# Folding the token mixing's gain and bias into the weights: one multiply from PSUM in place of a bias operation and a multiply

## The chip, the cores and the metric

The kernel runs on one core of a Trainium2 chip. The metric is the device time of one execution in microseconds (us). Most executions of one kernel agree within some tenths of a per cent, so medians of several runs are compared, and a run that is more than 1.5% above the fastest of its kernel counts as slow and is left out of the ratios.

The engines are called PE (matrix multiplies), PEld (PE's weight loads), DVE (vector), ACT (scalar), POOL (GpSimd) and SP (it issues most transfers). PE writes to PSUM; DVE and ACT read PSUM or SBUF; POOL works in SBUF here. The *granted clock* of PE is the share of its full clock that it was given, as the profile shows it.

## The reference

A retention layer (attention without softmax, with a decay per head) feeds a gated MLP whose gate mixes tokens. Shapes: batch 8, 8 heads, 576 tokens, head size 64, so the model size is 512 and the MLP's half width is 512.

```python
# retention: x[b, t, :] = sum_{s<=t} gamma_h^(t-s) (q_t . k_s)/sqrt(64) v_s, heads side by side
h = gelu_tanh(x @ w_in);  u, v = halves of h
v_n = (v - mean(v)) / sqrt(var(v) + 1e-6) * g_ln
v_s = einsum('ts,bsd->btd', w_sg, v_n) + b_sg[None, :, None]
out = x + (u * v_s) @ w_out                  # float32
```

What matters: `g_ln` scales a feature and `b_sg` is added to a token. With S = w_sg · normalised v, the gated value is u · (g_f S_tf + b_t).

## The kernel before

The 8 × 576 tokens are cut into 36 tiles of 128. Two batch items make nine tiles, so the fifth tile of each pair (`m == MID`) holds 64 tokens of either item. The mixing matrix is transposed once into `wT[e][j]`, with zero rows where the shared tile holds the other item's tokens. The retention of tile i+1, the projections of tile i and, from a work list, two pieces of "later" work run in each step: a piece is one token mixing (`mlp_W`, 32 pieces, four feature blocks for each item) or one output projection (`mlp_O`, 36 pieces).

```python
def prep(i):                                             # POOL: casts and decay-scaled values
    nc.gpsimd.tensor_copy(qkb[:], qk[:]...)              # f32 -> bf16, 128x1024
    for hh in range(2):
        nc.gpsimd.tensor_tensor(vp[...], vf[...], gv[...], op=Alu.mult)
    ...
def mlp_V(i):
    ...                                                  # hv on PE, vg = gelu on ACT, statistics on DVE and POOL
    vn = vnp.tile([128, F2], BF, name="vn")
    nc.scalar.activation(vn[:], vg[:], Act.Identity, scale=rs[:], bias=nm[:])
    vns[i] = vn
    ...
def mlp_W(b, c):
    ...
    ps = [psD.tile([128, HS], F32, name="wp", tag="d") for _ in range(2)]
    for j in range(SB):                                  # 5 token tiles
        for half in range(2):
            nc.tensor.matmul(ps[half][:], vns[t0 + j][:, 128 * c:128 * c + 128],
                             wT[e][j][:, half * HS:(half + 1) * HS],
                             start=(j == 0), stop=(j == SB - 1))
    for half in range(2):
        col = e * S + half * HS
        vs = work.tile([128, HS], BF, name="vs")
        nc.vector.scalar_tensor_tensor(vs[:], ps[half][:], g_col[:, c:c + 1],
                                       b_bc[:, half * HS:(half + 1) * HS],
                                       op0=Alu.mult, op1=Alu.add)
        nc.vector.tensor_tensor(gTs[p][:, c, col:col + HS], vs[:], uTs[p][:, c, col:col + HS], op=Alu.mult)
    ...
def mlp_O(i):
    ...                                                  # op = gT @ w_out + x, on PE
    nc.scalar.activation(ob[:], op[:], Act.Copy)         # ACT empties PSUM
    nc.scalar.dma_start(outf[128 * i:128 * i + 128, :], ob[:])
```

The three PSUM buffers of `psD` are shared by hv, hu, wp and op. In names: sc holds the scores of a tile and ret their masked form; vpad holds v with its decay; zp and zbd are the state that goes from one tile to the next; xT is the retention's result, transposed. hu and hv are the halves of x @ w_in before gelu, uT and vg after it; nm, rs and vn belong to the normalisation; wp is a mixing, op an output projection.

Of the kernel before, what the change touches and what calls it, by code (L numbers as in the profile page):

```python
# [11 lines left out]
F32 = mybir.dt.float32  # L12
BF = mybir.dt.bfloat16
I32 = mybir.dt.int32
Act = mybir.ActivationFunctionType
Alu = mybir.AluOpType
# [3 lines left out]
def kernel(  # L20
# [12 lines left out]
    nc = tc.nc  # L33
    B, H, S, D = q.shape
    DM = H * D
    F2 = moe_w_in.shape[1] // 2
    KK = H // 2
    NT = 2 * S // 128
    NP = B // 2
    MID = NT // 2  # L40
    HS = S // 2
    SB = (S + 127) // 128
# [4 lines left out]
    consts = ctx.enter_context(tc.tile_pool(name="consts", bufs=1))  # L47
    ld = ctx.enter_context(tc.tile_pool(name="ld", bufs=5))
    work = ctx.enter_context(tc.tile_pool(name="work", bufs=4))
    pairp = ctx.enter_context(tc.tile_pool(name="pairp", bufs=2))  # L50
    vnp = ctx.enter_context(tc.tile_pool(name="vnp", bufs=14))
    psA = ctx.enter_context(tc.tile_pool(name="psA", bufs=1, space=bass.MemoryType.PSUM))
    psS = ctx.enter_context(tc.tile_pool(name="psS", bufs=2, space=bass.MemoryType.PSUM))
    psD = ctx.enter_context(tc.tile_pool(name="psD", bufs=3, space=bass.MemoryType.PSUM))
# [12 lines left out]
    def load(i):  # L67
        p, m = divmod(i, NT)
        qk = ld.tile([128, 2, H, D], F32, name="qk", tag="qk")
        vf = ld.tile([128, H, D], F32, name="vf")  # L70
        for (p0, b, r0, n) in segs(m):
            bb = 2 * p + b
            nc.sync.dma_start(qk[p0:p0 + n, 0, :, :], q[bb, :, r0:r0 + n, :].transpose([1, 0, 2]))
            nc.sync.dma_start(qk[p0:p0 + n, 1, :, :], k[bb, :, r0:r0 + n, :].transpose([1, 0, 2]))
            nc.sync.dma_start(vf[p0:p0 + n, :, :], v[bb, :, r0:r0 + n, :].transpose([1, 0, 2]))
        loaded[i] = (qk, vf)
# [4 lines left out]
    w_in = consts.tile([128, KK, 2 * F2], BF, name="w_in")  # L81
    w_out = consts.tile([128, KK, DM], BF, name="w_out")
    wnat = consts.tile([128, SB, S + 128], BF, name="wnat")
    b_bc = consts.tile([128, S], F32, name="b_bc")
    g_col = consts.tile([128, KK], F32, name="g_col")
    w_stage = []
    for half in (1, 0):
        for c in (0, 2):
            wst = ld.tile([128, 2, F2], F32, name="wst", tag="qk")
            nc.sync.dma_start(wst[:], moe_w_in.rearrange("(c p) f -> p c f", p=128)[:, c:c + 2, half * F2:(half + 1) * F2])  # L90
            w_stage.append((half, c, wst))
        load(1 if half else 2)
    nc.sync.dma_start(b_bc[:], moe_b_sg.partition_broadcast(128))
    nc.sync.dma_start(g_col[:], moe_g_ln.rearrange("(c p) -> p c", p=128))


    ident = consts.tile([128, 128], BF, name="ident")
# [6 lines left out]
    NB0 = S - 128 * MID  # L104
# [36 lines left out]
    kbds = [consts.tile([128, KK, 2, 128], BF, name=f"kbd{i}") for i in range(NK)]  # L141
    zbds = [consts.tile([128, KK, 128], BF, name=f"zbd{i}") for i in range(NZ)]
    kmid = consts.tile([128, H * D], BF, name="kmid")
    for t in vpads[:1] + kbds[:1] + vpads[1:] + kbds[1:] + zbds:
        nc.vector.memset(t[:], 0.0)
    nc.vector.memset(kmid[:NB0, :], 0.0)

    def load_w():
        nc.gpsimd.memset(wnat[:, :, 0:64], 0.0)
        nc.gpsimd.memset(wnat[:, :, 64 + S:], 0.0)  # L150
        for j in range(SB):
            n = min(128, S - 128 * j)
            nc.gpsimd.dma_start(wnat[:n, j, 64:64 + S], moe_w_sg[128 * j:128 * j + n, :])
        nc.gpsimd.dma_start(w_out[:], moe_w_out.rearrange("(c p) f -> p c f", p=128))


    wT = [[consts.tile([128, S], BF, name=f"wT{e}_{j}") for j in range(SB)] for e in range(2)]
# [11 lines left out]
    xTs, uTs, gTs = {}, {}, {}  # L169
    zp = {}  # L170

    def prep(i):
        p, m = divmod(i, NT)
        qk, vf = loaded.pop(i)
        qkb = work.tile([128, 2, H * D], BF, name="qkb")
        nc.gpsimd.tensor_copy(qkb[:], qk[:].rearrange("p a h d -> p a (h d)"))  # L176
        vp = vpads[i % NV]
        for hh in range(2):
            nc.gpsimd.tensor_tensor(
                vp[:].rearrange("p (k g) c -> p k g c", g=2)[:, :, hh, hh * 64:hh * 64 + 64],  # L180
                vf[:].rearrange("p (k g) d -> p k g d", g=2)[:, :, hh, :],
                gv[:, m, :].rearrange("p (k g) -> p k g", g=2)[:, :, hh].unsqueeze(2).to_broadcast([128, KK, 64]),
                op=Alu.mult)
        if m == MID:
            nc.gpsimd.tensor_copy(kmid[NB0:, :], qk[NB0:, 1, :, :].rearrange("p h d -> p (h d)"))
        st[i] = dict(qkb=qkb, vp=vp)
# [73 lines left out]
    vns = {}  # L260

    def mlp_V(i):
        p, m = divmod(i, NT)
        hv = psD.tile([128, F2], F32, name="hv", tag="d")
        for kk in range(KK):
            nc.tensor.matmul(hv[:], xTs[p][:, kk, 128 * m:128 * m + 128], w_in[:, kk, F2:],  # L266
                             start=(kk == 0), stop=(kk == KK - 1))
        vg = work.tile([128, F2], F32, name="vg")
        nc.scalar.activation(vg[:], hv[:], Act.Gelu_apprx_tanh)  # L269
        bst = work.tile([128, 6], F32, name="bst")  # L270
        nc.vector.bn_stats(bst[:], vg[:])  # L271
        mv = work.tile([128, 2], F32, name="mv")
        nc.vector.bn_aggr(mv[:], bst[:])  # L273
        rs = work.tile([128, 1], F32, name="rs")
        nc.gpsimd.tensor_scalar(rs[:], mv[:, 1:2], 1e-6, None, op0=Alu.add)  # L275
        nc.gpsimd.tensor_tensor(rs[:], rs[:], mhalf[:], op=Alu.pow)  # L276
        nm = work.tile([128, 1], F32, name="nm")
        nc.gpsimd.tensor_scalar(nm[:], mv[:, 0:1], rs[:], -1.0, op0=Alu.mult, op1=Alu.mult)  # L278
        vn = vnp.tile([128, F2], BF, name="vn")
        nc.scalar.activation(vn[:], vg[:], Act.Identity, scale=rs[:], bias=nm[:])  # L280
        vns[i] = vn

    def mlp_U(i):
        p, m = divmod(i, NT)
# [10 lines left out]
    def mlp_W(b, c):  # L295
        p, e = divmod(b, 2)
        if e == 0 and c == 0:
            gTs[p] = pairp.tile([128, KK, NT * 128], BF, name="gT")
        t0 = NT * p + (MID if e else 0)
        ps = [psD.tile([128, HS], F32, name="wp", tag="d") for _ in range(2)]  # L300
        for j in range(SB):
            for half in range(2):
                nc.tensor.matmul(ps[half][:], vns[t0 + j][:, 128 * c:128 * c + 128],  # L303
                                 wT[e][j][:, half * HS:(half + 1) * HS],
                                 start=(j == 0), stop=(j == SB - 1))
        for half in range(2):
            col = e * S + half * HS
            vs = work.tile([128, HS], BF, name="vs")
            nc.vector.scalar_tensor_tensor(vs[:], ps[half][:], g_col[:, c:c + 1],  # L309
                                           b_bc[:, half * HS:(half + 1) * HS],  # L310
                                           op0=Alu.mult, op1=Alu.add)
            nc.vector.tensor_tensor(gTs[p][:, c, col:col + HS], vs[:], uTs[p][:, c, col:col + HS], op=Alu.mult)  # L312

    def mlp_O(i):
        p, m = divmod(i, NT)
        op = psD.tile([128, DM], F32, name="op", tag="d")
        r = slice(128 * m, 128 * m + 128)
        for c in range(KK):
            nc.tensor.matmul(op[:], gTs[p][:, c, r], w_out[:, c, :], start=(c == 0), stop=False,  # L319
                             skip_group_check=True)  # L320
        for kk in range(KK):
            nc.tensor.matmul(op[:, 128 * kk:128 * kk + 128], xTs[p][:, kk, r], ident[:],  # L322
                             start=False, stop=True, skip_group_check=True)
        ob = work.tile([128, DM], F32, name="ob")
        nc.scalar.activation(ob[:], op[:], Act.Copy)  # L325
        nc.scalar.dma_start(outf[128 * i:128 * i + 128, :], ob[:])  # L326
# [5 lines left out]
    def run(n):  # L332
        for _ in range(n):
            if wo:
                wo.pop(0)()
# [7 lines left out]
    def flush(i):  # L343
        while waiting and waiting[0][0] <= i:
            b = waiting.pop(0)[1]
            p, e = divmod(b, 2)
            lo = NT * p + (MID if e else 0)
            for c in range(KK):
                wo.append(lambda b=b, c=c: mlp_W(b, c))
            for m in range(MID + e):  # L350
                wo.append(lambda i=lo + m: mlp_O(i))
# [9 lines left out]
    wbuild = [(e, j) for e in range(2) for j in range(SB)]  # L361
    for i in range(N + 3):
        flush(i)
        if i + 4 < N:
            load(i + 4)
        if i + 2 < N:
            prep(i + 2)
        if i < N:
            attn_S(i)
        if 1 <= i <= N:  # L370
            mlp_V(i - 1)
            release(i - 1)
        if i >= 2 and wbuild:
            build_wT(*wbuild.pop(0))
            build_wT(*wbuild.pop(0))
        if i + 1 < N:
            attn_T(i + 1)
        if 1 <= i <= N:
            mlp_U(i - 1)
        if i < N:  # L380
            attn_O(i)
            attn_Z(i)
        run(2)
# [31 lines left out]
```

## Time and profile before

| Before | |
|---|---|
| time, median of the first 3 runs | 283.47 us (282.51 to 283.56) |
| profiled span | 280.1 us, mean granted PE clock 0.982 |
| busy | PE 225.7, DVE 204.5, ACT 127.5, POOL 126.2 us |
| 12 steps with two mixings, while input work goes on ("W steps") | 84.27 us, 7.02 each |
| 12 steps with two projections | 78.46 us, 6.54 each |
| 3 steps with one projection | 17.05 us |
| seventh xT write, where the first mixings come in | at 66.50 us |
| last xT write, then the drain | at 257.85 us, 22.2 us |

A *step* is the time from one xT write on DVE to the next, read off the timeline; its kind is given by the gT writes in it. Steps let one cut the span where different things limit it.

Busy times by engine (first part of the page of the kernel before; us, share of the span, instructions):

```profile
PE 225.7 (81%) x2462; PEld 171.4 (61%) x2498; DVE 204.5 (73%) x451; ACT 127.5 (46%) x226; POOL 126.2 (45%) x240
```

No engine is busy for the whole span, so the total alone does not name a limit. A window of two W steps does. The columns are busy time with the number of records for each engine, then the granted PE clock, the transfers' share and their rate (windows of the kernel before; the first line heads the columns):

```profile
core 0: us, PE busy (x) PEld busy (x) DVE busy (x) ACT busy (x) POOL busy (x), PEclk, DMA share, GB/s
125.98:140.82 14.84, 11.72 (x131) 9.07 (x131) 14.78 (x32) 5.36 (x9) 8.81 (x15) 1.00 1.13 196
```

DVE is busy 14.78 of 14.84 us: these steps are DVE's. This pair is heavier than the mean of 7.02 us a step; over all twelve W steps DVE is busy 83.8 of 84.27 us. (PE's 131 records are fewer than the 144 matmuls that two such steps issue: the weight loads, of which none is missing, number 131 too, so PE had run ahead of xT and did most of the others before the window. Of hv's eight matmuls the trace has six.)

The costliest groups on DVE (page of the kernel before; line, engine, operation, tiles and shapes, count, then busy us and mean ns, then idle time just before them and what ended it):

```profile
L212 DVE TENSOR_TENSOR ret<-sc,tri 128x512 bf16<-128x512 f32 x64 | 40.9, 678 | 6.5 <-PE sc L210 6.5
...
L309 DVE SCALAR_TENSOR_TENSOR vs<-wp,g_col,b_bc 128x288 bf16<-128x288 f32 x64 | 29.8, 503 | 2.8 <-PE wp L303 2.6
...
L312 DVE TENSOR_TENSOR gT<-vs,uT 128x288 bf16<-128x288 bf16 x64 | 28.1, 477 | 0.0
```

The gate's multiply, gT, has a mean of 477 ns, but the mean hides two populations. The view of the tile gT gives minimum, median and maximum:

```profile
L312 DVE TENSOR_TENSOR gT<-vs,uT x64: 289/301/1144, 67.5 to 271.7; 128x288 bf16<-128x288 bf16 x64
```

The slow ones are found where POOL reads SBUF. First DVE's timeline, then POOL's, for the same stretch (start us, duration us, engine, line, operation; x2 is two instructions drawn as one):

```profile
187.26 0.92 DVE L309 SCALAR_TENSOR_TENSOR vs<-wp,g_col,b_bc 128x288 bf16<-128x288 f32 x2
188.12 1.36 DVE L312 TENSOR_TENSOR gT<-vs,uT 128x288 bf16<-128x288 bf16 x2
```

```profile
187.64 1.03 POOL L176 CAST qkb<-qk 128x1024 bf16<-128x1024 f32 x1
188.65 1.30 POOL L179 TENSOR_TENSOR vpad_157<-vf,gv 128x256 bf16<-128x256 f32 x2
```

Two multiplies that take 0.51 us elsewhere (at 163.46 us in the same trace; their records overlap a little) take 1.36 us beside POOL's cast and multiplies; vs, whose second tensor is in SBUF but whose first is in PSUM, keeps its 0.92 us for two. The Trainium skill, "SBUF — State Buffer", section "Who interferes with whom", says that a DVE instruction with two SBUF inputs contends with a GpSimd instruction that reads SBUF, and that one with at most one SBUF input (outside the two-port modes) does not. The trace agrees.

How DVE's load reaches PE is in the waits (kernel before; who waited for whom, us in total, times, longest):

```profile
PE wp L303 <- DVE vs L309: 7.7, 11, 1.0
```

### The profile page before, as it was taken

To read this page: it belongs to the slowest core of one execution; us is meant where nothing else is said; L and a number is where in the kernel's file an instruction comes from. 1 tells how busy PE (TensorE), PEld (TensorE's weight loads), DVE (VectorE), ACT (ScalarE), POOL (GpSimd) and SP (SyncE) were. 2 spreads that over 40 slices of the span, in tenths; PEclk is the share of its full clock that TensorE was granted. 3 is DMA by queue.
4 is the path that set the end of the run, shared out by engine and by line. 5 is a ranking of instruction groups with operands and counts; after the bars stand their busy time and mean duration, and the time that the engine had idled before them with its cause. 6 is when DMAs were issued, how large, how long until landed. Compare 5 with 4: busy or idle time off the path is not lost.

```text
span 280.1 us, 6362 instructions
## 1 busy us (share of the span) xinstructions
PE 225.7 (81%) x2462; PEld 171.4 (61%) x2498; DVE 204.5 (73%) x451; ACT 127.5 (46%) x226; POOL 126.2 (45%) x240
## 2 busy tenths in 40 slices
PE   0428773879889889986898799887997999889894
PEld 0216553657667667765676577666766777667562
DVE  7826672749996797579965997679876986599170
ACT  1632443223346536553455345563356455644613
POOL 5923518057455545646615665365634561111200
PEclk9999996879999999999999999999999999999999
DMA  8999999993005896699939897799945002200304
GB/s 183 256 282 196 169 201 205 224 208 77 21 0 148 205 211 155 152 257 211 186 97 220 159 202 189 195 172 170 205 130 136 0 2 80 90 23 1 116 37 187
DMA packets 120670, 41.74 MB, mean 149 GB/s; under 512 B 113792, under 2 KB 114880, under 8 KB 120640
## 3 DMA queue, kind: packets, MB, share of 16 engines
q1 hardware_dynamic: 114272, 30.71, 57.0%
q10 hardware_dynamic: 5184, 9.44, 9.1%
q0 software_dynamic: 1184, 1.19, 2.5%
q8 instruction: 19, 0.31, 0.5%
q14 instruction: 11, 0.09, 0.1%
HBM read 33.08 MB, written 9.44 MB: 152 GB/s over the span
## 4 chain that ended last, share of the span: by engine, by line
DVE 39%; PE 24%; ACT 10%; DMA 7%; POOL 7%; issue 6%; SPq 3%; ACTq 2%; POOLq 0%; DVEq 0%
DVE gT L312 7%; DVE ret L212 7%; DVE vs L309 7%; PE op L319 7%; DVE bst L271 5%; ACT ob L325 5%; DMA vf<-in_v_dram 5%; DVE xT L234 4%; ACT vg L269 3%; PE hv L266 3%; PE hu L290 2%; ACTq L326 2%; PE ot L230 2%; PE sc L210 2%; PE wp L303 2%
## 5 line engine op out<-in xcount | busy, mean ns | idle before, releaser
L275 POOL TENSOR_SCALAR rs<-mv 128x1 f32<-128x1 f32 x36 | 8.0, 221 | 114.7 <-DVE mv L273 114.6
L280 ACT ACTIVATE vn<-vg,nm,rs 128x512 bf16<-128x512 f32 x36 | 29.3, 814 | 55.1 <-POOL nm L278 55.1
L271 DVE BATCH_NORM_STATS2 bst<-vg 128x6 f32<-128x512 f32 x36 | 24.7, 687 | 30.7 <-ACT vg L269 30.7
L212 DVE TENSOR_TENSOR ret<-sc,tri 128x512 bf16<-128x512 f32 x64 | 40.9, 678 | 6.5 <-PE sc L210 6.5
L290 PE MATMUL hu<-xT,w_in 128*128 128x128 bf16 x576 | 38.7, 220 | 4.5 <-ACT ob L325 3.8
L303 PEld LDWEIGHTS <-vn 128*128 128x128 bf16 x320 | 30.2, 97 | 19.3 <-issue 11.7
L176 POOL CAST qkb<-qk 128x1024 bf16<-128x1024 f32 x36 | 37.3, 1035 | 9.2 <-DMA qk<-in_k_dram 6.4
L266 PE MATMUL hv<-w_in,xT 128*128 128x512 bf16 x123 | 36.8, 390 | 4.8 <-DVE xT L234 2.7
L290 PEld LDWEIGHTS <-w_in 128*128 128x128 bf16 x576 | 34.7, 98 | 7.4 <-issue 5.8
L269 ACT ACTIVATE vg<-hv 128x512 f32<-128x512 f32 x36 | 21.5, 596 | 37.4 <-PE hv L266 30.5
L319 PE MATMUL op<-w_out,gT 128*128 128x512 bf16 x129 | 35.9, 379 | 0.6
L309 DVE SCALAR_TENSOR_TENSOR vs<-wp,g_col,b_bc 128x288 bf16<-128x288 f32 x64 | 29.8, 503 | 2.8 <-PE wp L303 2.6
L193 PE MATMUL tp<-ident,qkb 128*128 128x128 bf16 x288 | 23.9, 230 | 9.3 <-POOL qkb L176 9.3
L193 PEld LDWEIGHTS <-qkb 128*128 128x128 bf16 x288 | 20.2, 103 | 17.3 <-POOL qkb L176 9.7
L312 DVE TENSOR_TENSOR gT<-vs,uT 128x288 bf16<-128x288 bf16 x64 | 28.1, 477 | 0.0
L293 ACT ACTIVATE uT<-hu 128x512 bf16<-128x512 f32 x36 | 21.3, 590 | 11.3 <-PE hu L290 11.3
L325 ACT ACTIVATE ob<-op 128x512 f32<-128x512 f32 x36 | 20.9, 591 | 11.2 <-PE op L322 7.5
L234 DVE TENSOR_TENSOR xT<-ot,ttab 128x512 bf16<-128x512 f32 x36 | 24.4, 677 | 1.6 <-PE ot L230 1.0
L195 DVE COPY qT<-tp 128x512 bf16<-128x512 bf16 x36 | 14.8, 412 | 11.3 <-PE tp L193 11.1
L276 POOL TENSOR_TENSOR rs<-rs,mhalf 128x1 f32<-128x1 f32 x36 | 20.4, 566 | 2.8
L266 PEld LDWEIGHTS <-xT 128*128 128x128 bf16 x144 | 12.6, 101 | 12.1 <-DVE xT L234 3.9
L319 PEld LDWEIGHTS <-gT 128*128 128x128 bf16 x144 | 12.6, 98 | 8.6
(109 smaller groups left out, 432.8 us busy)
## 6 DMA issues: line engine op xcount, KB each, us to landing
out_dram<-ob ACTq DMA_DIRECT2D x36, 256.0 KB, 2.4
qk<-in_q_dram SPq DMA_DIRECT2D x32, 256.0 KB, 5.1
qk<-in_k_dram SPq DMA_DIRECT2D x32, 256.0 KB, 5.0
vf<-in_v_dram SPq DMA_DIRECT2D x32, 256.0 KB, 5.0
wst<-in_moe_w_in_dram SPq DMA_DIRECT2D x4, 512.0 KB, 8.5
qk<-in_q_dram SPq DMA_DIRECT2D x8, 128.0 KB, 4.8
qk<-in_k_dram SPq DMA_DIRECT2D x8, 128.0 KB, 4.6
vf<-in_v_dram SPq DMA_DIRECT2D x8, 128.0 KB, 4.4
```

What stands on the lines that cost most here:

```text
L176: nc.gpsimd.tensor_copy(qkb[:], qk[:].rearrange("p a h d -> p a (h d)"))
L193: nc.tensor.transpose(tp[:, a, kk, :], s["qkb"][:, a, kk * 128:(kk + 1) * 128], ident[:])
L212: nc.vector.tensor_tensor(ret[:, 4 * j:4 * j + 4, :], sc[:], msk[:].unsqueeze(1).to_broadcast([128, 4, 128]), op=Alu.mult)
L234: nc.vector.tensor_tensor(xTs[p][:, :, 128 * m:128 * m + 128], ot[:], ttab[:, :, t0:t0 + 128], op=Alu.mult)
L266: nc.tensor.matmul(hv[:], xTs[p][:, kk, 128 * m:128 * m + 128], w_in[:, kk, F2:], start=(kk == 0), stop=(kk == KK - 1))
L271: nc.vector.bn_stats(bst[:], vg[:])
L290: nc.tensor.matmul(hu[:, c, :], w_in[:, kk, 128 * c:128 * c + 128], xTs[p][:, kk, 128 * m:128 * m + 128], start=(kk == 0), stop=(kk == KK ...
L303: nc.tensor.matmul(ps[half][:], vns[t0 + j][:, 128 * c:128 * c + 128], wT[e][j][:, half * HS:(half + 1) * HS], start=(j == 0), stop=(j == ...
L309: nc.vector.scalar_tensor_tensor(vs[:], ps[half][:], g_col[:, c:c + 1], b_bc[:, half * HS:(half + 1) * HS], op0=Alu.mult, op1=Alu.add)
L312: nc.vector.tensor_tensor(gTs[p][:, c, col:col + HS], vs[:], uTs[p][:, c, col:col + HS], op=Alu.mult)
L319: nc.tensor.matmul(op[:], gTs[p][:, c, r], w_out[:, c, :], start=(c == 0), stop=False, skip_group_check=True)
L325: nc.scalar.activation(ob[:], op[:], Act.Copy)
```

## The change

Intent: u·(g S + b) = g·u·(S + b/g). The factor g goes into the rows of `w_out`, once, at the start. The term b_t/g_f is a product of a column of 1/g and a row of b, so PE can add it as part of the mixing: the shared tile has zero rows in its contraction, and four of them are filled with b on the side of `wT` and 1/g on the side of `vn`. Four, because both numbers are split into a bf16 part and the bf16 rest, and all four products are summed. The shared tile therefore needs a normalised copy for each of the two items (`vmid`), each with its own four rows. What is left of the gating on DVE is one multiply that reads the mixing straight from PSUM.

```diff
-    vnp = ctx.enter_context(tc.tile_pool(name="vnp", bufs=14))
+    vnp = ctx.enter_context(tc.tile_pool(name="vnp", bufs=10))
 ...
-    nc.sync.dma_start(b_bc[:], moe_b_sg.partition_broadcast(128))
+    nonzero(g_col[:], g_tmp[:])                      # 3 DVE ops: |g| < 1e-20 becomes 3e-20
 ...
+    def build_rows():                                # called at step i == SB
+        nonzero(row4[:, 0, :F2], row_t[:, :F2])
+        nc.vector.reciprocal(row4[:, 0, :F2], row4[:, 0, :F2])
 ...                                                  # bf16 part or rest, by row, into row4b
+        for t in vmid:
+            nc.sync.dma_start(t[0][NB0:NB0 + 4, :], row4b[:, 0, :F2])
+            nc.sync.dma_start(t[1][0:4, :], row4b[:, 0, :F2])
+        nc.sync.dma_start(wT[0][SB - 1][NB0:NB0 + 4, :], row4b[:, 1, :])
+        nc.sync.dma_start(wT[1][0][0:4, :], row4b[:, 1, :])
 ...
-        nc.gpsimd.dma_start(w_out[:], moe_w_out.rearrange("(c p) f -> p c f", p=128))
+        for c in (0, 2):
+            wst = ld.tile([128, 2, F2], F32, name="wst", tag="qk")
+            nc.sync.dma_start(wst[:], moe_w_out.rearrange("(c p) f -> p c f", p=128)[:, c:c + 2, :])
+            for r in range(2):
+                nc.vector.tensor_scalar(w_out[:, c + r, :], wst[:, r, :], g_col[:, c + r:c + r + 1], None, op0=Alu.mult)
 ...
-        vn = vnp.tile([128, F2], BF, name="vn")
-        nc.scalar.activation(vn[:], vg[:], Act.Identity, scale=rs[:], bias=nm[:])
-        vns[i] = vn
+        if m == MID:
+            vns[i] = vmid[p % 2]
+            for e, sl in ((0, slice(0, NB0)), (1, slice(NB0, 128))):
+                nc.scalar.activation(vns[i][e][sl, :], vg[sl, :], Act.Identity, scale=rs[sl, :], bias=nm[sl, :])
+        else:
+            vn = vnp.tile([128, F2], BF, name="vn")
+            nc.scalar.activation(vn[:], vg[:], Act.Identity, scale=rs[:], bias=nm[:])
+            vns[i] = [vn, vn]
 ...
-            vs = work.tile([128, HS], BF, name="vs")
-            nc.vector.scalar_tensor_tensor(vs[:], ps[half][:], g_col[:, c:c + 1],
-                                           b_bc[:, half * HS:(half + 1) * HS],
-                                           op0=Alu.mult, op1=Alu.add)
-            nc.vector.tensor_tensor(gTs[p][:, c, col:col + HS], vs[:], uTs[p][:, c, col:col + HS], op=Alu.mult)
+            nc.vector.tensor_tensor(gTs[p][:, c, col:col + HS], ps[half][:], uTs[p][:, c, col:col + HS], op=Alu.mult)
```

## The prediction

> **What bounds it now.** The page gives PE 81% busy, DVE 73%, ACT 46%, POOL 45%; no engine bounds the whole span. By the timeline, a step is the time from one xT write (L234) to the next. Steps with two token mixings ("W steps", L309/L312) took 6.4 to 7.6 us, twelve of them 84 us between 66 and 228 us. There DVE is the limit: 17.6 to 18.1 us busy of 20 in the windows at 60, 120 and 180 us, and PE waits up to 1.0 us for a wp buffer held by vs (waits: PE wp from DVE vs, 7.7 us). Output-projection steps took 5.7 to 7.0 us, set by PE, ACT and few PSUM buffers. After 228 us, when POOL has no input work left, the same W steps take 5.7 and 5.9 us.
>
> **Removed, by groups of instructions.** vs: 64 x 503 ns = 29.8 us. gT: 64 x 477 ns = 28.1 us, although its fastest take 289 ns and its slowest 1144 ns; the slow ones coincide with POOL casts and multiplies. The Trainium skill, "SBUF — State Buffer", section "Who interferes with whom", says that a DVE instruction with two SBUF inputs contends with a GpSimd instruction that reads SBUF; this trace agrees (ret and xT, with one PSUM input each, keep to 670-692 and 647-693 ns).
>
> **Added.** 64 multiplies with one PSUM input. ret and xT have that form, 512 wide, 678 ns; I estimate 440 ns for 288 wide (pitch about 0.4 us), uncontended: 28 us. So DVE loses about 30 us net. PE: nothing; the spare rows make no matmul longer. ACT: the middle tile's normalisation becomes two instructions of 0.8 us, +3.3 us in all. POOL: four memsets at the start. DVE once: w_out scaling about 1.6 us, zero repair and row building about 5 us. A few row copies by DMA; w_out moves to the sync queue in f32; the b broadcast (0.29 MB) goes.
>
> **On the critical path.** A W step's DVE work drops from about 7 us to about 5.3 us. PE then binds: the pitches of its groups sum to 6.0 us. I expect W steps of 6.1 us: 12 x (7.0 - 6.1) = about -10.5 us. The last two barely gain; the drain's mixings gain 0.7 us. Split ACT work costs +1 us. The start costs +2 us (0 to 6): g_col landed only at 27 us, its repair and the w_out scaling sit in DVE's in-order stream in a latency-bound phase (steps of 6.4 to 11.9 us), and the first mixing must wait for the rows. So 30 us of removed work gives only about 8 us.
>
> **Prediction:** 275.3 us, 8 in 10 between 268 and 281. Faster by over 2% 0.70, within 2% 0.26, slower 0.04.
>
> **What would show each step right.** gT at 420 to 480 ns with hardly any spread; DVE busy about 180 us, PE near 226; mid-run W steps near 6.1 us, with PE's waits for wp buffers mostly gone; output steps unchanged; the first mixing 0 to 6 us later than 63 us.
>
> **What would make it wrong.** A schedule in which DVE stalls at the start on g_col or the w_out load for more than 6 us; a row DMA queued behind loads; W steps that stay near 6.7 us because the wait moves to ACT's chain (hv, vg, statistics, vn); or output steps gaining too, which would take it under 268.

## The result, and the profile after

| | before | after |
|---|---|---|
| median of 4 runs each, same rounds | 283.51 us (282.51 to 284.43) | 274.66 us (273.36 to 277.48, the last one slow) |
| ratio of fast runs | 1 | 0.9673 (95% interval 0.9611 to 0.9735) |
| profiled span | 280.1 us | 272.1 us |
| 12 W steps | 84.27 us | 74.19 us |
| last two W steps (no input work left) | 11.57 us | 11.50 us |
| 12 two-projection steps | 78.46 us | 77.66 us |
| 3 one-projection steps | 17.05 us | 20.17 us |
| seventh xT write | at 66.50 us | at 66.08 us |
| last xT write to the end | 22.21 us | 22.46 us |

A ratio is the mean time of one kernel's fast runs over that of the other's of the same rounds, so it is not quite the ratio of the medians quoted. Each ratio below is against the kernel before, run in the same rounds on the same chip. The changed kernel is correct and 3.3% faster. Its own runs spread more than those of the kernel before, in two clumps, 273.1 to 273.9 and 275.4 to 276.3 us (with those of r1_after_again, below).

The step table adds up to the profiled difference: −10.1 (W steps) −0.1 (last two) −0.8 (two projections) +3.1 (one projection) −0.4 (start) +0.25 (drain) = −8.0 us, and 272.1 − 280.1 = −8.0.

First part of the page, changed kernel:

```profile
PE 227.3 (84%) x2498; PEld 171.3 (63%) x2498; DVE 189.2 (70%) x405; ACT 130.1 (48%) x230; POOL 128.1 (47%) x244
```

DVE's busy time fell by 15.3 us. The two old groups summed to 57.9 us and the new one sums to 26.1 us, 31.8 less; neighbouring DVE instructions overlap in their records, so a group's sum is more than its share of busy time, and one-time work was added (below). Two W steps of the changed kernel (windows; columns as before):

```profile
125.37:137.33 11.96, 10.78 (x131) 8.71 (x129) 10.27 (x24) 5.33 (x10) 7.46 (x14) 1.00 1.08 204
```

14.84 us became 11.96, and DVE now has 1.7 us of slack in it. The same stretches restricted to the gating give DVE 8.14 us busy before (vs and gT) and 3.25 us after (gT): 4.9 us less work for 2.9 us less time. From about 6.0 us a step on, something else is the limit: the pitches of PE's instructions (from the start of one to the start of the next) in such a step sum to 6.0 us in the trace of before, and the 12 W steps of the best variant below averaged 5.99 us. PE's own work is not all of it. No matmul is missing from this trace (2498 records), and in these 11.96 us PE is idle for 1.18 us. 1.06 us of that comes near the start, where it waits for a wp buffer until gT, which stands behind xT and zbd on DVE, has read it; from there to the end of the pair PE's pauses sum to 0.12 us.

A new order of instructions on PE is a rival that the traces rule out for most of the run: by tile names, the 2498 weight loads of the two kernels stand in the same order from the 540th (about 80 us) to the 2461st (the drain). Before and after that, 157 of them stand elsewhere, so the first two W steps are not covered.

The groups on DVE (page of the changed kernel):

```profile
L253 DVE TENSOR_TENSOR ret<-sc,tri 128x512 bf16<-128x512 f32 x64 | 41.0, 682 | 10.9 <-PE sc L251 10.9
...
L354 DVE TENSOR_TENSOR gT<-wp,uT 128x288 bf16<-128x288 f32 x64 | 26.1, 448 | 11.3 <-PE wp L349 11.3
```

DVE now idles 11.3 us before gT, waiting for PE's wp; before, it idled 2.8 us there. The view of the tile gT:

```profile
L354 DVE TENSOR_TENSOR gT<-wp,uT x64: 439/448/459, 71.6 to 262.6; 128x288 bf16<-128x288 f32 x64
```

The spread is gone: 439 to 459 ns, with POOL's casts as frequent as before. Note that 448 ns is *more* than the 289 to 301 ns of an undisturbed multiply before. The Trainium skill, "VectorE: DVE Perf Modes", section "The perf-mode tier table", gives a tensor_tensor of bf16 from SBUF two elements a cycle and any PSUM operand one; the trace agrees in direction. So the change gave up a fast form of the multiply for one that POOL cannot disturb.

The waits of PE for a mixing buffer (changed kernel):

```profile
PE wp L349 <- DVE gT L354: 5.9, 6, 1.1
```

They fell only from 7.7 us (11 times) to 5.9 us (6 times).

Where the 3.1 us came in: a one-projection step holds the normalisation of the shared tile, which is now two ACT instructions. ACT's timeline in the kernel before:

```profile
121.70 0.81 ACT L280 ACTIVATE vn<-vg,nm,rs 128x512 bf16<-128x512 f32 x1 [1.88 <-POOL nm L278]
122.54 0.38 ACT L252 ACTIVATE zbd_160<-zp 64x256 bf16<-64x256 f32 x1
```

and in the changed kernel:

```profile
120.21 0.81 ACT L323 ACTIVATE vmid_175<-vg,nm,rs 64x512 bf16<-64x512 f32 x1 [2.45 <-POOL nm L319]
121.04 0.81 ACT L323 ACTIVATE vmid_176<-vg,nm,rs 64x512 bf16<-64x512 f32 x1
121.87 0.38 ACT L293 ACTIVATE zbd_170<-zp 64x256 bf16<-64x256 f32 x1
```

Half the partitions take the same 0.81 us, so the split doubles the work, and zbd, which the next retention needs on PE, stands behind it. PE's timeline, changed kernel, with its idle time and releaser in brackets:

```profile
122.30 0.23 PE L267 MATMUL ot<-qT,zbd_170 128*128 128x128 bf16 x1 [0.94 <-ACT zbd_170 L293]
```

### The profile page after: what moved, and what is told of

Its sections match the earlier page's. It is cut to its first block, busy times and chain, and to the rows that moved or that the text cites. A ratio compares the mean times of both kernels' runs of the same rounds, so it can differ in the third digit from the quotient of the medians.

```text
span 272.1 us, 6371 instructions
## 1 busy us (share of the span) xinstructions
PE 227.3 (84%) x2498; PEld 171.3 (63%) x2498; DVE 189.2 (70%) x405; ACT 130.1 (48%) x230; POOL 128.1 (47%) x244
## 4 chain that ended last, share of the span: by engine, by line
PE 39%; DVE 22%; ACT 11%; DMA 8%; POOL 7%; issue 6%; SPq 3%; ACTq 2%; POOLq 0%; DVEq 0%
PE hv L307 7%; PE wp L349 6%; PE op L361 6%; PE hu L336 5%; DVE bst L312 5%; DMA vf<-in_v_dram 4%; ACT ob L367 4%; DVE xT L275 4%; ACT vg L310 4%; PE tp L234 3%; PE sc L251 3%; PE ot L271 3%; POOL rs L317 2%; ACTq L368 2%; DVE kbd_169 L239 2%
## 5 line engine op out<-in xcount | busy, mean ns | idle before, releaser
L326 ACT ACTIVATE vn<-vg,nm,rs 128x512 bf16<-128x512 f32 x32 | 26.0, 814 | 50.7 <-POOL nm L319 50.7
L307 PE MATMUL hv<-w_in,xT 128*128 128x512 bf16 x144 | 40.3, 398 | 3.8 <-DVE xT L275 3.7
L361 PE MATMUL op<-w_out,gT 128*128 128x512 bf16 x144 | 36.9, 379 | 0.0
L349 PEld LDWEIGHTS <-vn 128*128 128x128 bf16 x256 | 24.4, 97 | 18.9 <-issue 11.8
L354 DVE TENSOR_TENSOR gT<-wp,uT 128x288 bf16<-128x288 f32 x64 | 26.1, 448 | 11.3 <-PE wp L349 11.3
L367 ACT ACTIVATE ob<-op 128x512 f32<-128x512 f32 x36 | 21.1, 592 | 11.2 <-PE op L364 7.2
L307 PEld LDWEIGHTS <-xT 128*128 128x128 bf16 x144 | 12.5, 101 | 12.9 <-DVE xT L275 5.2
L364 PEld LDWEIGHTS <-xT 128*128 128x128 bf16 x144 | 11.1, 98 | 8.4
```

Source lines behind the costliest of these rows:

```text
L307: nc.tensor.matmul(hv[:], xTs[p][:, kk, 128 * m:128 * m + 128], w_in[:, kk, F2:], start=(kk == 0), stop=(kk == KK - 1))
L349: nc.tensor.matmul(ps[half][:], vns[t0 + j][e][:, 128 * c:128 * c + 128], wT[e][j][:, half * HS:(half + 1) * HS], start=(j == 0), stop=(j ...
L354: nc.vector.tensor_tensor(gTs[p][:, c, col:col + HS], ps[half][:], uTs[p][:, c, col:col + HS], op=Alu.mult)
L361: nc.tensor.matmul(op[:], gTs[p][:, c, r], w_out[:, c, :], start=(c == 0), stop=False, skip_group_check=True)
```

## The experiments

The theory after the result: *what counts in a W step is DVE's summed time against PE's 6.0 us* ("Theory C" in the expectation of f3). Rivals: (A) it is the removed instruction, vs, that gave the gain; (B) it is the removed contention between gT and POOL. A third of the questions is where the changed kernel lost: the start, and the split on ACT. Twelve kernels ran, in three groups; each group shared its runs of the kernel before (11 runs; medians 283.21, 283.58 and 282.82 us).

| run | correct | median us (range) | ratio to before (95%) | 12 W | 3 one-proj. | 12 two-proj. |
|---|---|---|---|---|---|---|
| e1_dead_op | yes | 278.62 (276.11–280.12) | 0.9817 (0.9761–0.9874) | 75.32 | 19.50 | 79.68 |
| e2_before_quiet_pool | no | 270.99 (269.61–272.28) | 0.9572 (0.9526–0.9619) | 74.90 | 17.38 | 79.00 |
| e3_after_quiet_pool | no | 273.23 (272.39–274.07) | 0.9636 (0.9599–0.9674) | 74.63 | 19.74 | 77.04 |
| e4_half_on_pool | yes | 273.97 (273.26–275.96) | 0.9672 (0.9636–0.9708) | 74.15 | 17.67 | 77.30 |
| r1_after_again | yes | 274.42 (273.11–276.26) | 0.9689 (0.9645–0.9732) | 74.18 | 20.14 | 77.36 |
| f1_rows_on_act_queue | yes | 269.92 (268.44–270.71) | 0.9517 (0.9484–0.9550) | 71.92 | 19.51 | 76.99 |
| f2_rows_and_half | yes | 269.90 (267.34–271.14) | 0.9510 (0.9470–0.9551) | 71.95 | 17.04 | 76.78 |
| f5_and_ob_on_dve | yes | 261.89 (259.35–263.69) | 0.9250 (0.9208–0.9292) | 71.94 | 16.06 | 71.45 |
| f3_vs_in_psum | yes | 283.41 (282.38–284.88) | 1.0021 (0.9982–1.0059) | 85.65 | 17.18 | 73.59 |
| g2_before_ob_on_dve | yes | 274.80 (272.90–276.01) | 0.9727 (0.9686–0.9767) | 83.49 | 16.07 | 71.39 |
| g3_rows_and_ob | yes | 261.64 (261.31–263.52) | 0.9265 (0.9232–0.9297) | 71.92 | 18.52 | 72.03 |
| e4_look_again | yes | 273.29, one run | – | 74.17 | 17.65 | 77.40 |

The three right columns are us, summed over the steps of each kind, from the profile of each run.

### e1_dead_op: the changed kernel with a short dead instruction before each multiply

```diff
         for half in range(2):
             col = e * S + half * HS
+            vs = vs_dead
+            nc.vector.scalar_tensor_tensor(vs[:, :144], ps[half][:, :144], g_col[:, c:c + 1], ttab[:, 0, :144],
+                                           op0=Alu.mult, op1=Alu.add)
             nc.vector.tensor_tensor(gTs[p][:, c, col:col + HS], ps[half][:], uTs[p][:, c, col:col + HS], op=Alu.mult)
```

Its result is read by nobody.

> The changed kernel, with one dead DVE instruction put back ahead of each gating multiply: 144 wide, one PSUM input and one SBUF input, result never read (result stays correct). It has no second SBUF input to contend with POOL. It costs about 0.28 us of DVE pitch, so vs and an uncontended gT together are imitated (about 0.68 us a half) without contention. Theory A (DVE's load in the W steps was the limit and any DVE instruction there costs time): W steps go from a mean of 5.97 us to about 6.4 to 6.6 us, the twelve of them +5 to +8 us, total 279 to 283 us. Rival B (only the contention with POOL mattered; PE binds while DVE has slack, so a short uncontended instruction is free): W steps stay below 6.1 us, total 274 to 276 us.

Measured (view of the tile vs_dead, and the window of two W steps):

```profile
L356 DVE SCALAR_TENSOR_TENSOR vs_dead<-wp,g_col,ttab x64: 333/349/368, 74.7 to 268.8; 128x144 bf16<-128x144 f32 x64
```

```profile
128.72:140.69 11.97, 10.82 (x130) 8.90 (x130) 11.90 (x32) 5.36 (x9) 8.49 (x15) 1.00 1.06 181
```

DVE's slack filled up (11.90 of 11.97 us busy) and the steps stayed at 6.28 us, against 6.18. So a half-width vs, 22.4 us in sum over 64 instructions, fits into the slack almost without cost there: the part of the removed vs that it stands for had bought no time in these steps. The ten W steps after the first two, where the start still shows, took 60.38 us against 59.77. Neither expectation was met in full: 6.28 us lies between "below 6.1" and "6.4 to 6.6", and so does the total between the two ranges. The total is 4 us worse than the changed kernel's, but the W steps hold only 1.1 us of that. The seventh xT came at 69.25 us instead of 66.08, and the two-projection steps took 2.0 us more. In this build some 260 of PE's 4998 instructions also stand in another place than in the changed kernel, so the total's 4 us are not the dead instruction's price alone.

### e2_before_quiet_pool and e3_after_quiet_pool: POOL's casts and multiplies shrunk, in both kernels

From the fifth tile on, the cast takes 16 columns of each half instead of 512, and the multiply of v 8 of 64 columns (from the sixth). The tiles keep stale data, so the result is wrong; the instructions, waits and transfers stay.

```diff
-        qkb = work.tile([128, 2, H * D], BF, name="qkb")
-        nc.gpsimd.tensor_copy(qkb[:], qk[:].rearrange("p a h d -> p a (h d)"))
+        if i < 4:
+            qkbs.append(consts.tile([128, 2, H * D], BF, name=f"qkb{i}"))
+        qkb = qkbs[i % 4]
+        w = H * D if i < 4 else 16
+        nc.gpsimd.tensor_copy(qkb[:, :, :w], qk[:].rearrange("p a h d -> p a (h d)")[:, :, :w])
 ...                                                  # and n = 64 if i < NV else 8 columns of v
```

> The kernel before, with POOL's input work cut down on purpose (wrong result): from the fourth or fifth tile on, the cast of q and k is 16 columns wide per half instead of 512, the multiply of v 8 columns wide per head instead of 64. PE, ACT and DVE instructions are unchanged. Theory B (contention of the two-SBUF-input gT with POOL's reads gives most of the gain): gT falls from 477 to about 300 ns mean, W steps from 7.0 to 5.8 to 6.0 us, total 270 to 273 us, as good as the change. Theory A (the separate vs instruction is the main cost): W steps only fall to 6.4 to 6.7 us, total 277 to 281 us.

> Control for the run before: the changed kernel with POOL's input work cut down in the same way (wrong result). If contention and nothing else ties POOL to the W steps, this does nothing to W steps (5.9 to 6.0 us) and the total stays within 273 to 276 us. If POOL's work holds up other things (the start, or nm and vn), the total falls by some us, and that much has to be taken off what the run before seems to show.

Measured on the kernel before with a quiet POOL (view of the tile gT, and two W steps):

```profile
L318 DVE TENSOR_TENSOR gT<-vs,uT x64: 285/291/627, 63.6 to 259.3; 128x288 bf16<-128x288 bf16 x64
```

```profile
120.79:132.85 12.06, 10.78 (x130) 8.79 (x130) 12.00 (x32) 5.36 (x9) 3.44 (x13) 1.00 1.09 192
```

With vs still in place, the removed contention alone brings the W steps from 7.02 to 6.24 us, nearly as far as the whole change did (6.18). DVE is full in both (14.78 of 14.84, and here 12.00 of 12.06); its work in these two steps fell by 2.8 us, to PE's length. PE's weight loads stand in the order of the kernel before but for 40 of 2498, all before 90 us. In e3, where gT cannot contend, a quiet POOL moved nothing in the W steps (74.63 against 74.19 us).

The comparison of e2 and e3 is telling: with a quiet POOL, the changed kernel is *not* faster than the kernel before (273.23 against 270.99 us; the intervals of the ratios overlap a little). e2's total also has an earlier start, its seventh xT at 62.64 us against 66.50 in the kernel before and 66.43 in e3, so not all of its gain is contention in W steps. From the seventh xT to the end the profiles of e2 and e3 take the same time, 205.1 and 205.4 us.

Rival A fails: the gain in the W steps is there with vs still in place. Rival B explains the same gain, so one more run had to separate it from the theory.

### f3_vs_in_psum: the kernel before, without contention and without saving DVE time

```diff
-            vs = work.tile([128, HS], BF, name="vs")
+            vs = ps[half]
             nc.vector.scalar_tensor_tensor(vs[:], ps[half][:], g_col[:, c:c + 1],
```

vs is written back in place into PSUM. gT then has one SBUF input, as in the changed kernel.

> The kernel before, but vs is written back in place into its PSUM tile, and gT reads it from there (correct result): both instructions stay, and gT has one SBUF input only, so no contention. By the run of the kernel before with a quiet POOL, either saving alone brought the W steps to 6.2 us. Theory C (what counts is DVE's time in a W step, whether it is contention or an instruction; below about 6.2 us PE binds): DVE's pitches add up to 3.7 + 4 x (0.43 + 0.40) = 7.0 us, W steps stay at 6.8 to 7.2 us, total 280 to 285 us. Theory B (contention as such, whatever DVE's sum): W steps 6.2 to 6.4 us, total 272 to 276 us. The scheduler interleaves PE a little differently here, since wp is held longer.

Measured (view of the tile wp, two of its lines; then two W steps):

```profile
L309 DVE SCALAR_TENSOR_TENSOR wp<-wp,g_col,b_bc x64: 508/509/526, 68.6 to 273.2; 128x288 f32<-128x288 f32 x64
L312 DVE TENSOR_TENSOR gT<-wp,uT x64: 440/446/457, 70.0 to 274.0; 128x288 bf16<-128x288 f32 x64
```

```profile
126.75:140.49 13.74, 11.86 (x138) 9.38 (x138) 13.28 (x32) 5.36 (x9) 8.58 (x15) 1.00 1.14 193
```

The spread of gT is gone as in the changed kernel, and the time did not move: ratio 1.0021 (0.9982 to 1.0059). Without contention the multiply costs 446 ns where it averaged 477, so DVE's sum is nearly the same (203.5 us busy against 204.5). Rival B as a cause by itself fails: without any contention the W steps did not get shorter. (PE's order differs from the kernel before in some 900 rows here, so neither its split between kinds of steps nor its total is a clean comparison. Two of its twelve W steps took 8.55 us with DVE busy for 6.88, while five took 6.46 with DVE busy for 6.40.)

The last two W steps, where POOL has no input work in any of these kernels, say the same without POOL: they took 11.57 us in the kernel before (DVE busy 11.51), 11.50 in the changed kernel (9.98), and 13.21 in f3 (12.95), whose gT costs more than an undisturbed one.

Together, by the twelve W steps of each profile (sums of the windows view over the twelve windows, us):

| | 12 W steps | DVE busy in them |
|---|---|---|
| before | 84.27 | 83.8 |
| f3_vs_in_psum | 85.65 | 80.1 |
| e2_before_quiet_pool | 74.90 | 73.2 |
| e1_dead_op | 75.32 | 72.8 |
| changed kernel | 74.19 | 62.7 |
| e3_after_quiet_pool | 74.63 | 62.5 |

Bringing DVE's sum down to 73 us, about 6.1 us a step, gives the gain (e1, e2); 80 us gives none (f3); and the further 10 us that the changed kernel and e3 save give no more. A removed vs with the contention still there was not run; a gT that reads PSUM cannot have it.

### e4_half_on_pool and e4_look_again: the second half of the shared tile's normalisation on POOL

```diff
             for e, sl in ((0, slice(0, NB0)), (1, slice(NB0, 128))):
-                nc.scalar.activation(vns[i][e][sl, :], vg[sl, :], Act.Identity, scale=rs[sl, :], bias=nm[sl, :])
+                if e == 0:
+                    nc.scalar.activation(vns[i][e][sl, :], vg[sl, :], Act.Identity, scale=rs[sl, :], bias=nm[sl, :])
+                else:
+                    nc.gpsimd.tensor_scalar(vns[i][e][sl, :], vg[sl, :], rs[sl, :], nm[sl, :],
+                                            op0=Alu.mult, op1=Alu.add)
```

> The changed kernel with the second half of the middle tile's normalisation on POOL instead of ACT (correct result; PE's and DVE's order of instructions is unchanged). Theory: the second ACT instruction of 0.81 us stands in ACT's order before zbd, ob and vg, for which PE waits, so the single-projection step that holds it grew from 5.7 to 6.5 to 7.1 us three times. Then these steps go back to 5.7 to 5.9 us, total 2 to 3 us less: about 272 us, ratio to the changed kernel 0.990. Rival (the longer steps come from the new phase of the pipeline after faster W steps, not from this instruction): these steps stay at 6.5 us or more and the total stays within 0.3%.

> A second profile of the changed kernel with the middle tile's second half on POOL. In the first, its three single-projection steps were 2.5 us shorter in all, but the seventh xT came at 71.1 us, 5 us later than in the changed kernel, at a lower granted clock, and its times were no better. If that late start was the luck of one run, this one starts at 66 us and is 2.5 to 3 us faster than the changed kernel (271 us); if it belongs to the kernel, it starts at 68 us or later again.

The one-projection steps lost 2.5 us, from 20.17 to 17.67, which shows that 2.5 of the 3.1 us are the second ACT instruction. PE's order is the same as in the changed kernel. But the total hardly moved (0.9672 against 0.9673 and 0.9689), because the seventh xT came at 71.1 and 68.3 us. From there to the end the two profiles took 203.0 and 203.1 us, against 206.0 and 205.6 in the changed kernel and r1: the gain in the steps is there, and is lost before them. PE's timeline in the second shows where:

```profile
60.80 0.22 PE L289 MATMUL zp<-vpad,qkb 128*128 128x128 bf16 x1 [2.45 <-POOL vpad L220]
...
63.26 1.91 PE L340 MATMUL hu<-xT,w_in 128*128 128x128 bf16 x16
```

and the same in r1_after_again, the changed kernel run again:

```profile
59.57 0.22 PE L289 MATMUL zp<-vpad,qkb 128*128 128x128 bf16 x1 [1.44 <-POOL vpad L220]
...
61.57 1.06 PE L336 MATMUL hu<-xT,w_in 128*128 128x128 bf16 x16
```

POOL's extra instruction (0.77 us) stands before vpad, PE waits 1.0 us longer for vpad, and then the same sixteen matmuls take 1.91 us instead of 1.06: the granted clock in the window from 60 to 65 us was 0.73 here and 1.00 in r1. The Trainium skill, "TensorE: Matmul & The Clock Gate", Part 1, says that PE's clock is halved after an idle window of about 3.4 us and restored after a busy one; the wait shown, 2.45 us, is shorter than that. And e1_dead_op speaks against the wait as the cause: PE waited 1.44 us for vpad there, as in r1, and the sixteen matmuls took 1.91 us all the same (at 64.11 us; granted clock 0.50 from 60 to 65 us). What lowers the clock there stays open.

### r1_after_again: the changed kernel on the second group's chip

No edit.

> The changed kernel unaltered, timed again on the same chip as the three runs that follow, as their yardstick: 273 to 276 us.

0.9689 (0.9645 to 0.9732), against 0.9673 at first. The result repeats, and so do the two clumps: 273.1 to 273.4 and 275.4 to 276.3 us.

### f1_rows_on_act_queue and f2_rows_and_half: the first mixing

In the changed kernel the first mixing's matmuls on the shared tile came late. Two edits: the six row copies are issued from ACT's queue instead of SP's, and the two transposes that the rows are written into are made first.

```diff
         for t in vmid:
-            nc.sync.dma_start(t[0][NB0:NB0 + 4, :], row4b[:, 0, :F2])
-            nc.sync.dma_start(t[1][0:4, :], row4b[:, 0, :F2])
-        nc.sync.dma_start(wT[0][SB - 1][NB0:NB0 + 4, :], row4b[:, 1, :])
-        nc.sync.dma_start(wT[1][0][0:4, :], row4b[:, 1, :])
+            nc.scalar.dma_start(t[0][NB0:NB0 + 4, :], row4b[:, 0, :F2])
+            nc.scalar.dma_start(t[1][0:4, :], row4b[:, 0, :F2])
+        nc.scalar.dma_start(wT[0][SB - 1][NB0:NB0 + 4, :], row4b[:, 1, :])
+        nc.scalar.dma_start(wT[1][0][0:4, :], row4b[:, 1, :])
 ...
-    wbuild = [(e, j) for e in range(2) for j in range(SB)]
+    wbuild = [(0, SB - 1), (1, 0)] + [(0, j) for j in range(SB - 1)] + [(1, j) for j in range(1, SB)]
```

f2 has e4's edit as well.

> The changed kernel with its six row copies issued from ACT's queue instead of the sync queue, and the two weight tiles that receive rows transposed first, so that the copies do not wait for them (correct result). Theory: in the changed kernel the sync queue stood from 45.9 to 53.7 us at these copies, which waited for the rows and for the two transposed tiles, and DMA moved only 7 GB/s between 50 and 55 us; the loads behind them came late and the seventh and eighth tile waited. Then without it the DMA gap is gone, the seventh xT comes at 61 to 64 us instead of 66 us, total 271 to 273 us, ratio to the changed kernel 0.985 to 0.995. Rival (the start is bound by DVE's row building and the chain of dependences, the prefetch has room): the gap closes but the total stays within 0.3% of the changed kernel.

> As the run before, and in addition the second half of the middle tile's normalisation on POOL. If the two costs are independent, it gains another 2.5 us: 268.5 to 271 us, single-projection steps at 5.7 to 5.9 us.

The gain was larger than expected (274.42 to 269.92 us), and the reason that was given for it is refuted. It was to be the transfers: SP stood behind the row copies in the changed kernel, until 53.72 us, when it could issue the tenth tile's loads. In f1 SP has no row copies, but it still waits for them (waits of the queue of SP, 20 to 60 us):

```profile
SPq L73 <- DMA wT<-row4b: 12.5, 1, 12.5
```

and the tenth tile's loads went out even later, at 57.35 us (the seventh tile's at 47.40 instead of 34.03). The Trainium skill, "DMA: Bandwidth & Descriptors", section "Issuing engines are not separate DMA queues", says that issuing from several engines saves only the sequencer's time; no run here tests that, since SP held the loads back by a wait for the copies.

What the traces show instead is another order of PE's instructions, which is fixed when the kernel is built; about 160 of 4998 rows differ. PE's timeline of the changed kernel around the first mixing:

```profile
62.76 0.29 PE L349 MATMUL wp<-wT_0_191,vn 128*128 128x288 bf16 x1
...
71.24 0.53 PE L349 MATMUL wp<-wT_4_195,vmid_173 128*128 128x288 bf16 x3
...
72.68 1.03 PE L307 MATMUL hv<-w_in,xT 128*128 128x512 bf16 x4
```

and of f1:

```profile
63.22 0.29 PE L349 MATMUL wp<-wT,vn 128*128 128x288 bf16 x1
...
65.82 0.41 PE L349 MATMUL wp<-wT,vmid 128*128 128x288 bf16 x2
...
68.48 1.03 PE L307 MATMUL hv<-w_in,xT 128*128 128x512 bf16 x3
```

The first mixing starts at the same time in both, but its last matmuls, those of the shared tile, stand 5.4 us earlier in f1 (in the kernel before they ran at 65.63 us). Until then, by the program, the mixing holds two of the three PSUM buffers that hv needs too. The first two W steps took 14.42 us in the changed kernel and 12.16 us in f1. That is half of the measured 4.5 us; the rest is spread over later steps and over the start, where f1's six runs did not show the upper clump. f1 makes two edits at once, and no run parts them.

f2 has the one-projection steps back at 17.04 us, the level of before (17.05), and yet its total is that of f1 (269.90). As in e4, what was gained in those steps was not seen in the total, and its profile starts late too (seventh xT at 70.03 us, f1's at 66.62).

### f5_and_ob_on_dve, g2_before_ob_on_dve and g3_rows_and_ob: spend DVE's slack in the projection steps

The two-projection steps did not react to the change. ACT's order holds them up in part, so every other copy of the output out of PSUM was moved to DVE:

```diff
-        nc.scalar.activation(ob[:], op[:], Act.Copy)
+        if i % 2:
+            nc.vector.tensor_copy(ob[:], op[:])
+        else:
+            nc.scalar.activation(ob[:], op[:], Act.Copy)
```

f5 is f2 with this edit, g3 is f1 with it, g2 is the kernel before with it.

> As the run before, and in addition every other output tile is copied out of PSUM by DVE (0.65 us by the trace of ret and xT's width) instead of ACT. Theory: the projection steps are set by ACT's order (vn waits for nm, then zbd, ob, ob, vg) and PE waits for it, while DVE, relieved by the change, is busy for about 4.2 of their 6.4 us. Then the twelve two-projection steps fall from a mean of 6.45 to 5.9 to 6.1 us: -4 to -6 us, total 263 to 267 us. Rival (these steps are PE's own work, 5.7 us, plus DVE's chain of ret and statistics): they gain nothing or lose, total 269 to 273 us.

> The kernel before with nothing but every other output tile copied out of PSUM by DVE (correct result, PE's order unchanged). If the gain of that edit on the changed kernel (about 8 us, in projection steps) has nothing to do with what the change freed on DVE, since vs and gT run only in W steps, it shows here too: twelve projection steps from 78.5 to 72 to 73 us, total 275 to 278 us. If it needed the freed DVE, the total stays at 281 us or more.

> The changed kernel with its row copies on ACT's queue and every other output copy on DVE, but both halves of the middle tile's normalisation on ACT again (correct result). It tells whether the half on POOL is worth anything in the best version: by its steps alone it should be 2.5 us faster than this one, so 264 to 265 us here against 261.9; by the two timed runs that had it, which gained 0.2 us, this should be 261 to 263 us.

Page of g2 (kernel before, with the edit), and page of g3, first part:

```profile
PE 223.9 (83%) x2462; PEld 171.5 (63%) x2498; DVE 213.2 (79%) x469; ACT 118.0 (43%) x208; POOL 126.9 (47%) x240
```

```profile
PE 221.1 (85%) x2462; PEld 171.0 (66%) x2498; DVE 199.3 (77%) x423; ACT 120.5 (46%) x212; POOL 128.2 (49%) x244
```

The two-projection steps fell from 78.46 to 71.39 us on the kernel before and from 76.99 to 72.03 us on f1, although DVE, in those steps of the kernel before a little the busier engine (50 us against ACT's 49), got the work. The order of PE's instructions is unchanged by the edit (identical in g2 up to names; 4 rows in g3), so this is ACT's share and not a new schedule on PE. Which of ACT's instructions behind ob was the one waited for is not isolated. What is shown is that ACT's copies were on the critical path in steps where ACT was busy about 60% of the time.

This gain is nearly as large as the whole change (0.9727 by itself) and independent of it: f1's 0.9517 × 0.9727 = 0.9257, and g3 has 0.9265. f5's total is below its expected 263 to 267 us, since besides the twelve steps (−5.3 us against f2) the one-projection steps and the drain lost 1 us each. g3 is the best version: 261.64 us, 7.4% faster than the kernel before. f5 and g3 differ only in the half on POOL; 261.89 against 261.64 us says that it is worth nothing in the total.

## Why the prediction was right, and where a term was off

The predicted 275.3 us (268 to 281) met 274.66 us. Point by point:

- **What bounds the W steps: right.** DVE was busy 14.78 of 14.84 us before, and e1, e2 and f3 show from three sides that the W steps follow DVE's sum until it comes down to about 6.1 us a step.
- **30 us removed, 8 us gained: right, and for the reason given.** Predicted were −10.5 us in the W steps (to 6.1 us each); measured −10.1 us (6.18; 5.98 without the first two). Over the twelve steps DVE lost 21.1 us of busy time.
- **The new multiply at 440 ns, flat: right.** 439 to 459 ns, 26.1 us in sum.
- **Contention as part of the gain: right, but it is one of two ways to the same place.** The prediction added up both savings on DVE without saying that either of them alone would do. e2 showed that: the contention alone gave nearly the whole gain in the W steps (−9.4 of −10.1 us).
- **ACT's split, predicted +1 us: mis-sized, measured +3.1 us.** The instructions were costed well (2 × 0.81 us), but not their place. zbd stands behind them in ACT's order, and PE waited 0.94 us for it in the step shown. e4 confirmed it by taking 2.5 us back.
- **The start, predicted +2 us: −0.4 us in the profile.** The first mixing began at 62.76 us, against 63.0 before. The loss was elsewhere: the first two W steps took 14.42 us (14.77 before, 11.96 for a later pair), and the shared tile's matmuls came only at 71.24 us; f1 took 2.3 us of it back.
- **The drain, predicted −0.7 us: +0.25 us.** gT there waits for PE's wp, so a shorter DVE part buys nothing.
- **DVE busy about 180 us: 189.2.** The one-time work was 11.6 us instead of 6.6. One instruction stands out (groups by form, changed kernel):

```profile
L114 DVE RECIPROCAL row_111<-row_111 4x512 f32<-4x512 f32 x1 | 3.3, 3330 | 0.0
```

- **PE's waits for mixing buffers "mostly gone": no.** 7.7 us became 5.9. One wait of 0.65 to 1.06 us is left in each pair of W steps but the first: the buffer is now held until gT has read it, as before until vs had, and both stand behind xT and zbd in DVE's order.
- **Output steps unchanged: right for those with two projections** (78.46 to 77.66 us), wrong for those with one (+3.1 us).

The terms of the wrong sizes offset each other: start and drain together 1.5 us better than the sum predicted, ACT's split 2.1 us worse. That the total came within 1 us of the forecast is luck to that extent.

What is open: why runs of one kernel differ by 2 us in their start and in the granted clock there; which of f1's two edits makes its gain; why the half on POOL goes with a late start in three of its four profiles (f5's, at 65.81 us, is the exception), so that its shorter steps do not show in the total; and what behind ACT's copy the projection steps wait for.

## What to carry to other kernels

Cut the span into steps by what limits them, and count a saving only down to the next limit: here a quiet POOL alone brought the mixing steps to nearly the same floor as the whole change, and both together gave no more. A multiply with both inputs in SBUF beside POOL's casts can take two to four times as long, and reading one input from PSUM makes it even but slower than the undisturbed form, so it pays only if it removes another instruction as well. After such a change look for the engine with new slack and give it work of the engine that limits the other steps: moving half the output copies from ACT to DVE was worth nearly as much as the whole algebra, for a few lines.

## What the Trainium skill lacked or had wrong

- "VectorE: DVE Perf Modes" says that Reciprocal is an iterative divide with a repeat count of 8, but gives no duration. Here one of 4x512 f32 took 3.33 us, 6.5 ns for each element of a row, where a multiply with one PSUM input took 682 ns for 512.
- The same page's table for ScalarE (224 cycles plus the columns, SBUF to SBUF; an estimate of 613 ns for 512 at its 1.2 GHz) does not fit a normalisation with scale and bias from memory: 814 ns. "ScalarE: Activation LUTs" gives 280 ns plus 0.833 ns a column with one such operand and 93 ns for each further one, an estimate of about 800 ns: this fits, and the two pages differ.
- No page says that an ACTIVATE on 64 partitions takes as long as on 128: 0.81 us both, which is why the split doubled ACT's work.
- "SBUF — State Buffer" says that a multiply with two SBUF inputs contends with POOL's reads; it names factors of single probes, but no page sizes the cost in a running kernel. Here such a multiply averaged 477 ns instead of 308 ns (mean with a quiet POOL), with a worst case of 1144 ns.
